# A transformer block on one core: three-tile units from the start, and the weight scaling moved to GpSimd

## The chip, the core and the metric

The kernel runs on one core of one Trainium2 chip. The metric is the time of one execution on the device, in microseconds (us). The engines are named as in the profile: PE (TensorE), DVE (VectorE), ACT (ScalarE), POOL (GpSimd) and SP (SyncE).

## What is computed

Four batches of 768 rows, 8 heads of 64. Attention is local: rows come in chunks of 32, and a chunk sees 8 memory keys, its own chunk, 16 rows to the left and 8 to the right. Behind it stands a feed-forward block with a layer norm and a residual.

```python
# attention, per chunk c of 32 rows (batch 4, heads 8, seq 768, dim 64, n_mem 8)
k_full = concat([mem_k, k[c*32-16 : c*32+32+8]])
a = softmax(q_c @ k_full.T / 8);  out_c = a @ v_full
# feed-forward on x = attention output, [4, 768, 512]
xn = (x - mean(x)) / sqrt(var(x) + 1e-6) * g_ln
out = x + max(xn @ w_ch1, 0) @ w_ch2          # 512 -> 2048 -> 512
```

## The kernel before

**Tiles and units.** A tile is 128 rows, so a batch has 6 tiles and the whole has 24. Feed-forward work goes by units of up to three tiles. A unit `u` has 16 *ups* (`up`, L308: four matmuls of 128 x (128 n) for n tiles, then a relu to `rT` on DVE, L316, for even chunks and on ACT, L314, for odd ones) and then, for each tile, four *down* groups (`down`, L325: four matmuls 128x512 each); behind the last group DVE scales by `rstd` and adds the residual (L332, `osb`), and SP writes the tile out. Step by step this makes 16 + 4n steps.

**Attention of a tile.** `scores` (8 matmuls, then two exp on ACT, L236), `values` (16 matmuls, then on DVE a reciprocal, a multiply to `xs`, bn_stats, bn_aggr, and the centred `xn` on DVE or POOL), `turn_x` (four transposes on PE and a copy to `xT`, L296) and `root` (two POOL operations that make `rstd`). It runs one unit ahead: `attend` puts these calls at steps of unit `u` for the tiles of unit `u + 1`. Keys and queries come in as rows and are transposed on PE by `kq_block(b, j, ...)`, four blocks a batch: a *turn* of 32 transposes (L181), key copies to `KT` on DVE (L196), query copies to `QZ` on ACT (L206). `scores` needs all four blocks.

**What sets the order.** The schedule is written by hand: the code order is each engine's order, and the `at(step, ...)` table interleaves attention, turns and loads with a unit's steps. PSUM has two `att` buffers (scores, values, turns of x, most key/query turns) and four `mm` buffers (ups, downs), taken in rotation. Loads with a cast go through POOL's queue (`load_kq`, `load_v_group`, `load_w1`, `load_w2`); in this queue each DMA waits for the eighth one before it to land.

**The start.** Batch 0 is loaded in two parts (rows up to 64 of each 96-row group, then the rest). The units are

```python
    units = [[0, 1, 2], [3], [4], [5]] + [[t, t + 1, t + 2] for t in range(6, 6 * B, 3)]
```

so the rest of batch 0 goes in three units of one tile. The layer norm's `g_ln` is multiplied into `w1` by `scale_w1(c, q)`, four operations of 128x512 for each quarter: quarter (0,0) on ACT ahead of unit 0, the others on DVE at steps 1, 5 and 9 of unit 0. Chunks 4 to 7 of the ups read quarter (0,1), 8 to 11 (1,0), 12 to 15 (1,1). `clear_v(1)` and `clear_kq(1)`, memsets of the second buffers, stand at steps 11 and 13 of unit 0. The second half of batch 0's turns stands at steps 18 to 21 of unit 0, whose down groups go part by part over the tiles. Batch 1 is loaded from step 24 of unit 0 on, batch 2's keys and queries at the end of unit 3.

Of the kernel before, what the change touches and what calls it, by code (L numbers as in the profile page):

```python
# [10 lines left out]
ACTF = mybir.ActivationFunctionType  # L11
ALU = mybir.AluOpType
# [3 lines left out]
def kernel(  # L16
# [12 lines left out]
    nc = tc.nc  # L29

    B, H, S, D = 4, 8, 768, 64
    FF = 2048
    NG = 12
# [104 lines left out]
    def load_w2(c):  # L138

        nc.gpsimd.dma_start(  # L140
            out=w2c[c], in_=dram(moe_w_ch2, c * 512 * 512, [[2048, 128], [1, 2048]])
        )

    def scale_w1(c, q, on_act=False):

        for dt in range(4):
            w = w1c[c][:, dt, 512 * q : 512 * q + 512]
            if on_act:
                nc.scalar.activation(out=w, in_=w, func=ACTF.Copy, scale=g_col[:, dt : dt + 1])  # L149
            else:  # L150
                nc.vector.tensor_scalar(
                    out=w, in0=w, scalar1=g_col[:, dt : dt + 1], scalar2=None, op0=ALU.mult
                )


# [46 lines left out]
    def keep_q(copy, pv, b, j, par, n, g0, g1):  # L202


        rows = slice(64 * par, 64 * par + 64)
        copy(  # L206
            out=free(QZ[b % 2][rows, j, g0, par, :], 0, [[128, g1 - g0], [8, 8], [1, 8]]),
            in_=free(pv[rows, :], 8 * g0, [[8, g1 - g0], [1, 8], [n, 8]]),
        )
# [13 lines left out]
    def scores(b, t):  # L223
        p = slot("att")
        a = AT[t % 3]
        for gg in range(2):
            g = 2 * t + gg
            for j in range(4):
                nc.tensor.matmul(  # L229
                    out=p[:, gg, 128 * j : 128 * j + 128],  # L230
                    lhsT=KT[b % 2][:, j, KR * g : KR * g + 128],
                    rhs=QZ[b % 2][:, j, g, :, :],
                    start=True, stop=True,
                )
        for c in range(2):
            nc.scalar.activation(  # L236
                out=free(a, 32 * c, [[512, 2], [64, 8], [1, 32]], KR),
                in_=free(p, 32 * c, [[512, 2], [64, 8], [1, 32]], KR),
                func=ACTF.Exp, bias=band[0:KR, c : c + 1], scale=0.125,
            )  # L240
# [97 lines left out]
    def clear_kq(i):  # L338
        nc.vector.memset(KT[i][:, :, 8:24], 0.0)
        nc.vector.memset(KT[i][:, :, NG * KR - 8 : KC], 0.0)  # L340
        nc.vector.memset(QZ[i][0:64, :, :, 1, :], 0.0)
        nc.vector.memset(QZ[i][64:128, :, :, 0, :], 0.0)
# [33 lines left out]
    nc.scalar.copy(out=memk16, in_=memk32)  # L376
    clear_v(0)
    clear_kq(0)
    v_mem(0)
    for g in range(4):  # L380
        load_v_group(0, g)
# [16 lines left out]
    for g in range(6, 8):  # L398
        load_v_group(0, g)
    load_w2(2)  # L400
    load_w2(3)
    for g in range(8, NG):
        load_v_group(0, g)

    first_k = [as16(slot("mm")[:, :]) for j in range(4)]
# [20 lines left out]
    turn_x(0, 0, 0, nc.scalar.copy)  # L426
    values(0, 2, 2, False)
    turn_x(0, 1, 1, nc.scalar.copy)
    scale_w1(0, 0, True)
    turn_x(0, 2, 2, nc.scalar.copy)  # L430
    for t in range(3):
        root(t, t)


    units = [[0, 1, 2], [3], [4], [5]] + [[t, t + 1, t + 2] for t in range(6, 6 * B, 3)]
    for u, tiles in enumerate(units):
        n = len(tiles)
# [6 lines left out]
        def attend(*steps, on_pool=True):  # L444

            for i, (s0, s1, s2) in enumerate(steps):
                t = following[i]
                at(s0, scores, t // 6, t % 6)
                at(s1, values, t // 6, t % 6, t % 9, on_pool)
                at(s2, turn_x, u + 1, i, t % 6)  # L450
                if not on_pool:
                    at(s2, root, t % 6, t % 9)

        if u == 0:
            for c in range(1, 4):
                at(4 * c - 3, scale_w1, c // 2, c % 2)
            at(11, clear_v, 1)
            at(13, clear_kq, 1)
            for j in range(4):
                at(18 + j, kq_block, 0, j, 6, NG, "att")  # L460
            attend((21, 21, 24), on_pool=False)
            for which in range(2):
                at(24, load_kq, 1, which)
            for g in range(2):
                at(25, load_v_group, 1, g)
        elif u == 1:
            at(0, mem_cols, 1)
            at(0, v_mem, 1)
            attend((1, 16, 19), on_pool=False)
            for g in range(2, 6):  # L470
                at(19, load_v_group, 1, g)
        elif u == 2:
            attend((1, 6, 15), on_pool=False)
            for j in range(4):
                at(16 + j, kq_block, 1, j, 0, NG, "att")
            for g in range(6, NG):
                at(18, load_v_group, 1, g)
        elif u == 3:
            attend((1, 12, 16), (6, 16, 18), (14, 17, 19), on_pool=False)
            for which in range(2):  # L480
                at(19, load_kq, 2, which)
        elif following:
            steps = [(1 + 7 * i, 5 + 7 * i, 11 + 7 * i) for i in range(3)]
            attend(*steps)
            if u in (4, 6):
                b = u // 2
# [7 lines left out]
            if u == 5:  # L494
# [42 lines left out]
```

## Time and profile before

| | |
|---|---|
| Time of three runs | 265.8, 267.0, 269.39 us; median 267.0 |
| Profiled execution | 265.7 us, of which the trace spans 263.8 |
| Busy time of PE, DVE, ACT, POOL | 225.6, 144.3, 92.6, 77.1 us |
| Mean granted clock of PE | 0.974 |
| Moved by DMA | 22.04 MB |

Rows of the profile name line, engine, operation and `out<-in`; `xN` is a count. In a row of the timeline the first two numbers are the start and the duration, and brackets give the engine's idle time just before and what ended it. In a row of waits stand the total, the count and the longest.

### The profile page before, as it was taken

Reading aid. Unit: us, or ns where it says so; the run is one execution under the profiler, and the core shown is the slowest. Engines: PE = TensorE matmul, PEld = TensorE weight load, DVE = VectorE, ACT = ScalarE, POOL = GpSimd, SP = SyncE. Lnnn points to the kernel's source line nnn. Section 1 sums busy time; section 2 is a strip of 40 time slices with the busy share of each in tenths; the row PEclk is TensorE's granted clock in tenths of the full one; section 3 lists DMA queues with packets and bytes.
Section 4 is the critical chain, followed back from the end, with each engine's and each line's share of the span. In section 5 each row is a group of like instructions: output and inputs, shape, how many; then the busy total and the mean of one; then the engine's idle time right before and its main releaser. Section 6 shows DMA issues by size and latency. Waiting matters only on the chain.

```text
span 263.8 us, 5638 instructions
## 1 busy us (share of the span) xinstructions
PE 225.6 (86%) x2340; PEld 142.6 (54%) x2340; DVE 144.3 (55%) x323; ACT 92.6 (35%) x174; POOL 77.1 (29%) x149
## 2 busy tenths in 40 slices
PE   0555796959987778796999999999999999999993
PEld 0443363534755475474557745765576466546641
DVE  4729376324567728666566643677655446454321
ACT  2065331340422772252544511535455025302300
POOL 7750251006067002647130324274012202220000
PEclk9999999777999979999999999999999999999999
DMA  6999999005999900499989116079310120021012
GB/s 73 161 152 213 209 184 94 2 0 73 219 183 70 91 2 0 73 176 112 92 114 233 24 41 101 12 47 101 82 42 1 42 80 0 2 80 42 0 40 80
DMA packets 44104, 22.04 MB, mean 84 GB/s; under 512 B 32896, under 2 KB 39424, under 8 KB 44032
## 3 DMA queue, kind: packets, MB, share of 16 engines
q0 software_dynamic: 39312, 14.39, 66.4%
q1 hardware_dynamic: 4768, 7.31, 9.6%
q8 instruction: 18, 0.29, 0.5%
q14 instruction: 6, 0.05, 0.1%
HBM read 28.84 MB, written 6.29 MB: 133 GB/s over the span
## 4 chain that ended last, share of the span: by engine, by line
PE 66%; DVE 13%; DMA 8%; ACT 7%; issue 3%; POOL 1%; ACTq 0%; DVEq 0%; POOLq 0%
PE mm L325 29%; PE mm L308 26%; DMA q<-in_q_dram 8%; PE att L229 3%; PE att L181 3%; ACT QZ L206 3%; PE att L248 3%; ACT AT L236 2%; DVE KT L196 2%; DVE xs L256 2%; DVE bst L263 2%; PE att L291 1%; ACT w1c L149 1%; DVE xn L275 1%; DVE rT L316 1%
## 5 line engine op out<-in xcount | busy, mean ns | idle before, releaser
L308 PE MATMUL mm<-xT,w1c 128*128 128x384 f16 (+1 forms) x640 | 94.5, 302 | 5.3 <-DVE xT L296 1.9
L325 PE MATMUL mm<-w2c,rT 128*128 128x512 f16 x384 | 93.0, 390 | 2.1 <-DVE rT L316 2.1
L308 PEld LDWEIGHTS <-w1c 128*128 128x128 f16 x640 | 62.5, 116 | 28.2 <-issue 8.2
L314 ACT ACTIVATE rT<-mm 128x384 f16<-128x384 f32 (+1 forms) x80 | 33.4, 425 | 101.1 <-PE mm L308 66.7
L325 PEld LDWEIGHTS <-rT 128*128 128x128 f16 x384 | 36.0, 100 | 41.5 <-issue 5.7
L316 DVE TENSOR_SCALAR rT<-mm 128x384 f16<-128x384 f32 (+1 forms) x80 | 37.4, 474 | 36.0 <-PE mm L308 34.6
L206 ACT COPY QZ<-att 64x768 f16<-64x768 f16 (+1 forms) x33 | 21.9, 667 | 41.2 <-DVE KT L196 24.8
L236 ACT ACTIVATE AT<-att,band 96x512 f16<-96x512 f32 x48 | 30.1, 678 | 7.5 <-PE att L229 7.3
L332 DVE SCALAR_TENSOR_TENSOR osb<-mm,rstd,xs 128x512 f32<-128x512 f32 x24 | 18.0, 750 | 23.6 <-PE mm L325 18.8
L266 POOL TENSOR_SCALAR nmean<-mv 128x1 f32<-128x1 f32 x15 | 2.9, 191 | 83.9 <-DVE mv L264 76.1
L229 PE MATMUL att<-QZ,KT 128*128 128x128 f16 x192 | 16.7, 233 | 6.7 <-ACT QZ L206 4.7
L296 DVE COPY xT<-att 128x512 f16<-128x512 f16 x21 | 8.9, 423 | 24.5 <-PE att L291 24.5
L196 DVE COPY KT<-att 128x80 f16<-128x80 f16 (+3 forms) x38 | 16.2, 479 | 10.3 <-PE att L181 8.1
L281 POOL TENSOR_SCALAR veps<-mv 128x1 f32<-128x1 f32 x24 | 6.5, 270 | 51.0 <-DVE mv L264 49.6
L108 POOL DMA_DIRECT2D V<-in_v_dram x24 | 18.5, 778 | 6.9 <-DMA w2c<-in_moe_w_ch_dram 4.1
L229 PEld LDWEIGHTS <-KT 128*128 128x128 f16 x192 | 14.0, 105 | 9.1 <-issue 6.6
L263 DVE BATCH_NORM_STATS2 bst<-xs 128x6 f32<-128x512 f32 x24 | 16.7, 694 | 0.8
L256 DVE TENSOR_TENSOR xs<-att,rec 128x512 f32<-128x512 f32 x24 | 16.6, 691 | 0.8
L181 PEld LDWEIGHTS <-k 96*64 96x64 f16 (+1 forms) x320 | 8.5, 121 | 13.6 <-DMA k<-in_k_dram 8.5
L291 PE MATMUL att<-identity,xn 128*128 128x128 f16 x96 | 10.1, 233 | 5.0 <-DVE xn L275 4.3
L248 PEld LDWEIGHTS <-AT 96*64 96x64 f16 x384 | 8.9, 118 | 9.6 <-issue 4.4
L285 POOL TENSOR_TENSOR rstd<-veps,mhalf 128x1 f32<-128x1 f32 x24 | 13.4, 556 | 2.0
(52 smaller groups left out, 130.9 us busy)
## 6 DMA issues: line engine op xcount, KB each, us to landing
out_dram<-osb SPq DMA_DIRECT2D x24, 256.0 KB, 2.5
V<-in_v_dram POOLq DMA_DIRECT2D x36, 96.0 KB, 6.2
k<-in_k_dram POOLq DMA_DIRECT2D x3, 768.0 KB, 9.4
q<-in_q_dram POOLq DMA_DIRECT2D x3, 768.0 KB, 14.6
w1c<-in_moe_w_ch_dram POOLq DMA_DIRECT2D x2, 1024.0 KB, 14.0
w2c<-in_moe_w_ch_dram POOLq DMA_DIRECT2D x4, 512.0 KB, 16.5
k<-in_k_dram POOLq DMA_DIRECT2D x1, 512.0 KB, 6.2
q<-in_q_dram POOLq DMA_DIRECT2D x1, 512.0 KB, 8.9
```

The source lines that it names most:

```text
L108: nc.gpsimd.dma_start(out=V[b % 2][r : r + hi - lo, g, :, 0:64], in_=dram(v, b * H * HS + lo * D, [[64, hi - lo], [HS, H], [1, 64]]),)
L196: nc.vector.tensor_copy(out=free(KT[b % 2], j * KC + 24 + 32 * ga + 8 * lo, [[KR, gb - ga], [8, m], [1, 8]]), in_=free(pv, lo, [[8, gb - g ...
L206: copy(out=free(QZ[b % 2][rows, j, g0, par, :], 0, [[128, g1 - g0], [8, 8], [1, 8]]), in_=free(pv[rows, :], 8 * g0, [[8, g1 - g0], [1, 8], ...
L229: nc.tensor.matmul(out=p[:, gg, 128 * j : 128 * j + 128], lhsT=KT[b % 2][:, j, KR * g : KR * g + 128], rhs=QZ[b % 2][:, j, g, :, :], start ...
L236: nc.scalar.activation(out=free(a, 32 * c, [[512, 2], [64, 8], [1, 32]], KR), in_=free(p, 32 * c, [[512, 2], [64, 8], [1, 32]], KR), func= ...
L256: nc.vector.tensor_tensor(out=x.rearrange("p (a h d) -> p a h d", a=2, h=4), in0=free(p, 0, [[512, 2], [HD, 4], [1, 64]]), in1=free(r, 0, ...
L263: nc.vector.bn_stats(out=bst[i], in_=x)
L308: nc.tensor.matmul(out=p, lhsT=free(w, i, [[4, 128]]), rhs=xT[u % 2][:, dt, 0 : 128 * n], start=(dt == 0), stop=(dt == 3),)
L314: nc.scalar.activation(out=o, in_=p, func=ACTF.Relu)
L316: nc.vector.tensor_scalar(out=o, in0=p, scalar1=0.0, scalar2=None, op0=ALU.max)
L325: nc.tensor.matmul(out=p, lhsT=rT[hc][:, 128 * i : 128 * i + 128], rhs=w2c[hc // 4][:, hc % 4, :], start=(hc == 0), stop=(hc == 15),)
L332: nc.vector.scalar_tensor_tensor(out=o, in0=p, scalar=rstd[t % 9], in1=xs[t % 9], op0=ALU.mult, op1=ALU.add,)
```

## The change

Units are three tiles from the first to the last, so there are eight instead of ten. In unit 0 the second half of batch 0's turns comes at steps 14 to 17, the attention of tiles 3, 4 and 5 at steps 18 to 27, and the down groups go tile by tile. In unit 1 batch 1's turns stand at steps 2, 5, 8 and 11, and the attention of tiles 6, 7 and 8 at steps 13 to 26. Three quarters of `w1` are scaled on POOL, between the loads of its queue. `clear_kq(1)` and `clear_v(1)` move ahead of unit 0. Batch 1's keys, queries and first six V groups are issued behind the roots of tiles 0 to 2; its other V groups and batch 2's keys and queries at steps 0 and 1 of unit 1.

```diff
-    def scale_w1(c, q, on_act=False):
+    def scale_w1(engine, c, q):
         for dt in range(4):
             w = w1c[c][:, dt, 512 * q : 512 * q + 512]
-            if on_act:
-                nc.scalar.activation(out=w, in_=w, func=ACTF.Copy, scale=g_col[:, dt : dt + 1])
+            g = g_col[:, dt : dt + 1]
+            if engine is nc.scalar:
+                nc.scalar.activation(out=w, in_=w, func=ACTF.Copy, scale=g)
             else:
-                nc.vector.tensor_scalar(
-                    out=w, in0=w, scalar1=g_col[:, dt : dt + 1], scalar2=None, op0=ALU.mult
+                engine.tensor_scalar(
+                    out=w, in0=w, scalar1=g, scalar2=1.0, op0=ALU.mult, op1=ALU.mult
                 )
...
     clear_kq(0)
+    clear_kq(1)
...
     load_w2(2)
+    scale_w1(nc.gpsimd, 0, 1)
     load_w2(3)
-    for g in range(8, NG):
+    scale_w1(nc.gpsimd, 1, 0)
+    load_v_group(0, 8)
+    scale_w1(nc.gpsimd, 1, 1)
+    for g in range(9, NG):
         load_v_group(0, g)
...
+    clear_v(1)
     scores(0, 0)
...
-    scale_w1(0, 0, True)
+    scale_w1(nc.scalar, 0, 0)
...
+    for which in range(2):
+        load_kq(1, which)
+    for g in range(6):
+        load_v_group(1, g)
...
-    units = [[0, 1, 2], [3], [4], [5]] + [[t, t + 1, t + 2] for t in range(6, 6 * B, 3)]
+    units = [[t, t + 1, t + 2] for t in range(0, 6 * B, 3)]
...
         if u == 0:
-            for c in range(1, 4):
-                at(4 * c - 3, scale_w1, c // 2, c % 2)
-            at(11, clear_v, 1)
-            at(13, clear_kq, 1)
             for j in range(4):
-                at(18 + j, kq_block, 0, j, 6, NG, "att")
-            attend((21, 21, 24), on_pool=False)
-            for which in range(2):
-                at(24, load_kq, 1, which)
-            for g in range(2):
-                at(25, load_v_group, 1, g)
-        elif u == 1:
-            at(0, mem_cols, 1)
-            at(0, v_mem, 1)
-            attend((1, 16, 19), on_pool=False)
-            ...
-        elif u == 2:
-            attend((1, 6, 15), on_pool=False)
-            for j in range(4):
-                at(16 + j, kq_block, 1, j, 0, NG, "att")
-            ...
-        elif u == 3:
-            attend((1, 12, 16), (6, 16, 18), (14, 17, 19), on_pool=False)
-            for which in range(2):
-                at(19, load_kq, 2, which)
+                at(14 + j, kq_block, 0, j, 6, NG, "att")
+            attend(((18, 20, 23), (20, 22, 25), (22, 24, 27)), on_pool=False)
+            at(26, mem_cols, 1)
+            at(26, v_mem, 1)
+        elif u == 1:
+            for j in range(4):
+                at(2 + 3 * j, kq_block, 1, j, 0, NG, "att")
+            for g in range(6, NG):
+                at(0, load_v_group, 1, g)
+            for which in range(2):
+                at(1, load_kq, 2, which)
+            attend(((13, 16, 20), (16, 18, 23), (20, 22, 26)))
...
                 i, part = divmod(step - 16, 4)
-                if u == 0:
-                    part, i = divmod(step - 16, n)
                 down(tiles[i], i, part)
```

On POOL, in the prologue, the queue of loads stood so before (`w2c_77` and `w2c_78` are the third and fourth part of `w2`, `V_83` is the V buffer of batch 0, `veps` and `rstd` belong to the roots):

```order
L140 DMA w2c_77<-in_moe_w_ch_dram 128x2048
L140 DMA w2c_78<-in_moe_w_ch_dram 128x2048
L108 DMA V_83<-in_v_dram 96x8x64 x3
L108 DMA V_83<-in_v_dram 80x8x64
L281 TENSOR_SCALAR veps_137<-mv_128 128x1
```

and with the change:

```order
L140 DMA w2c_77<-in_moe_w_ch_dram 128x2048
L152 TENSOR_SCALAR w1c_73<-w1c_73,g_col 128x512 x4
L140 DMA w2c_78<-in_moe_w_ch_dram 128x2048
L152 TENSOR_SCALAR w1c_74<-w1c_74,g_col 128x512 x4
L108 DMA V_83<-in_v_dram 96x8x64
L152 TENSOR_SCALAR w1c_74<-w1c_74,g_col 128x512 x4
L108 DMA V_83<-in_v_dram 96x8x64 x2
L108 DMA V_83<-in_v_dram 80x8x64
L282 TENSOR_SCALAR veps_137<-mv_128 128x1
```

Twelve operations have come in, between loads that stay in their order.

On DVE, in the prologue, the memsets of the first key and query buffers (`KT_85`, `QZ_87`) stood directly ahead of the first key copies:

```order
L339 MEMSET KT_85 128x4x8
L340 MEMSET KT_85 128x4x20
L341 MEMSET QZ_87 64x48x32
L342 MEMSET QZ_87 64x48x32
L196 COPY KT_85<-mm_154 128x72
```

and with the change those of the second buffers (`KT_86`, `QZ_88`) stand between:

```order
L340 MEMSET KT_85 128x4x8
L341 MEMSET KT_85 128x4x20
L342 MEMSET QZ_87 64x48x32
L343 MEMSET QZ_87 64x48x32
L340 MEMSET KT_86 128x4x8
L341 MEMSET KT_86 128x4x20
L342 MEMSET QZ_88 64x48x32
L343 MEMSET QZ_88 64x48x32
L197 COPY KT_85<-mm_154 128x72
```

They came from step 13 of unit 0.

On DVE, at the end of unit 0, the attention of tile 3 (its `xn_101`), the turned x, and the three outputs stood ahead of the first relu of the next unit (`rT_106`, one tile wide):

```order
L275 TENSOR_SCALAR xn_101<-xs_95,mv_131 128x512
L296 COPY xT_105<-att_151 128x4x128
L332 SCALAR_TENSOR_TENSOR osb_122<-mm_155,rstd_140,xs_92 128x512
L332 SCALAR_TENSOR_TENSOR osb_123<-mm_156,rstd_141,xs_93 128x512
L332 SCALAR_TENSOR_TENSOR osb_124<-mm_153,rstd_142,xs_94 128x512
L316 TENSOR_SCALAR rT_106<-mm_154 128x128
```

and with the change, from the end of tile 4's attention (`xn_102`) on:

```order
L276 TENSOR_SCALAR xn_102<-xs_96,mv_132 128x512
L333 SCALAR_TENSOR_TENSOR osb_123<-mm_156,rstd_141,xs_93 128x512
L297 COPY xT_105<-att_152 128x4x128
L256 RECIPROCAL rec_150<-att_151 128x8
L257 TENSOR_TENSOR xs_97<-att_151,rec_150 128x512
L264 BN_STATS bst_127<-xs_97 128x6
L265 BN_AGGR mv_133<-bst_127 128x2
L276 TENSOR_SCALAR xn_103<-xs_97,mv_133 128x512
L297 COPY xT_105<-att_152 128x4x128
L172 COPY KT_86<-memKT 128x4x12x8
L333 SCALAR_TENSOR_TENSOR osb_124<-mm_153,rstd_142,xs_94 128x512
L297 COPY xT_105<-att_151 128x4x128
```

The last turned x, which the next unit's first up needs, now stands behind the attention of two more tiles and behind the third output.

More of the change, by code (lines that the diff above doesn't have):

```diff
@@ L442, in at, with attend @@
             plan.setdefault(step, []).append((fn, args))
-        def attend(*steps, on_pool=True):
+        def attend(steps, on_pool=True):
             for i, (s0, s1, s2) in enumerate(steps):
@@ L454 @@
         if u == 0:
[L455 to L458 removed]
             for j in range(4):
[L460 to L481 removed]
+                at(14 + j, kq_block, 0, j, 6, NG, "att")
[7 more added lines that the diff above has]
+                at(0, load_v_group, 1, g)
+            for which in range(2):
+                at(1, load_kq, 2, which)
+            attend(((13, 16, 20), (16, 18, 23), (20, 22, 26)))
         elif following:
             steps = [(1 + 7 * i, 5 + 7 * i, 11 + 7 * i) for i in range(3)]
[L484 to L486 removed]
+            attend(steps)
+            if u in (2, 4):
+                b = u // 2 + 1
                 for j, step in enumerate((steps[1][1], steps[2][1], steps[2][1], 23)):
@@ L493 @@
                 at(22, v_around, b)
-            if u == 5:
+            if u == 3:
                 for which in range(2):
```

## The prediction

> **What bounds the kernel now.** I read the page's head first, then a table of stages, then the waits inside the worst stages.
>
> ```profile
> span 263.8 us, 5638 instructions
> PE 225.6 (86%) x2340; PEld 142.6 (54%) x2340; DVE 144.3 (55%) x323; ACT 92.6 (35%) x174; POOL 77.1 (29%) x149
> GB/s 73 161 152 213 209 184 94 2 0 73 219 183 70 91 2 0 73 176 112 92 114 233 24 41 101 12 47 101 82 42 1 42 80 0 2 80 42 0 40 80
> ```
>
> TensorE (PE) is busy for 86% of the span, so the question is where the other 14% lies, and whether the busy time is at full speed. The table has one stretch for each unit (its length, then the busy time of PE, weight loads, DVE, ACT and POOL with their instructions, then the granted clock, the DMA share and GB/s):
>
> ```profile
> 28.48:65.90 37.42, 32.35 (x268) 17.86 (x268) 18.66 (x45) 8.97 (x18) 9.60 (x16) 0.86 0.81 87
> 65.90:75.80 9.90, 8.53 (x109) 6.12 (x108) 6.61 (x18) 3.15 (x10) 1.57 (x3) 1.00 1.40 217
> 75.80:90.00 14.20, 12.08 (x236) 8.94 (x235) 9.11 (x24) 6.53 (x15) 8.18 (x12) 1.00 1.49 92
> 90.00:108.75 18.75, 13.38 (x171) 9.73 (x166) 12.31 (x31) 8.61 (x18) 3.80 (x7) 0.91 0.05 16
> 108.75:138.19 29.44, 27.41 (x325) 17.43 (x325) 17.65 (x38) 13.67 (x22) 13.33 (x24) 1.00 1.74 125
> 138.19:162.62 24.43, 24.43 (x198) 14.84 (x197) 12.71 (x26) 7.49 (x14) 6.40 (x14) 1.00 0.51 98
> 162.62:190.06 27.44, 27.30 (x327) 17.37 (x325) 18.00 (x39) 13.67 (x22) 9.41 (x18) 1.00 0.65 69
> ```
>
> The prologue ends at 28.48. The rows are unit 0, the three one-tile units, then three-tile units, in which PE is idle for almost nothing. So the kernel is PE-bound from 108.75 on and chain-bound before. Tiles 0 to 5 take 37.42 + 9.90 + 14.20 + 18.75 = 80.27 us.
>
> What six tiles cost when PE is full follows from the last unit, which has no attention beside it:
>
> ```profile
> 238.62:249.01 10.39, 10.39 (x65) 7.26 (x64) 5.11 (x9) 3.44 (x7) 0.00 (x0) 1.00 0.07 27
> 249.01:259.40 10.39, 10.37 (x49) 4.51 (x46) 1.50 (x2) 0.49 (x1) 0.00 (x0) 1.00 0.14 50
> ```
>
> Ups and downs of three tiles are 20.8 us (0.162 us and 0.216 us per matmul). The unit at 138.19 adds the attention of three tiles: 24.43 - 20.8 = 3.65. The unit at 162.62 adds four key/query turns: 27.44 - 24.43 = 3.0. So a unit with three tiles, three attentions and four turns is **27.4 us**; two of them are 54.9, against 80.27. The gap of 25 us is what the change can reach for. It consists of waits such as these two of the end of unit 0, and of half clock:
>
> ```profile
> PE mm L325 <- DVE rT L316: 2.1, 1, 2.1
> PE att L229 <- ACT QZ L206: 1.4, 1, 1.4
> ```
>
> ```profile
> 42.54:45.95 3.41, 1.31 (x11) 0.43 (x11) 1.90 (x2) 0.00 (x0) 0.00 (x0) 1.00 1.75 36
> 45.95:49.36 3.41, 3.41 (x52) 1.91 (x51) 0.67 (x2) 0.95 (x2) 0.00 (x0) 0.54 0.00 0
> 79.90:83.30 3.40, 1.95 (x25) 1.41 (x23) 2.57 (x8) 0.83 (x3) 2.51 (x4) 1.00 0.90 32
> ```
>
> A stretch of 3.41 us with 1.31 us of PE work is followed by one at clock 0.54; the one with 1.95 us of work held 1.00 (the columns are those of the stages).
>
> **The prologue.** `clear_kq(1)` and `clear_v(1)` come into it, on VectorE (DVE).
>
> ```profile
> 4.28 0.09 DVE L339 MEMSET KT<- 128x32 uint32 x1
> 6.42 1.34 DVE L342 MEMSET QZ<- 64x1536 uint32 x1 [0.36 <-issue]
> 9.22 3.11 DVE L196 COPY KT<-mm 128x72 f16<-128x72 f16 x8 [1.47 <-PE mm L181]
> 13.58 0.56 DVE L206 COPY QZ<-att 64x384 f16<-64x384 f16 x1 [0.55 <-ACT QZ L206]
> 19.52 0.21 DVE L255 RECIPROCAL rec<-att 128x8 f32<-128x8 f32 x1 [3.43 <-PE att L248]
> 38.79 0.48 DVE L346 MEMSET V<- 32x512 f16 x1
> ```
>
> `clear_kq(0)` lasted from 4.28 to 7.76, 3.48 us; the second one is queued right behind it, ahead of the KT copies. DVE had 1.47 us free there and 0.55 us before its first QZ copy; the rest, 3.48 - 1.47 - 0.55 = **1.45 us**, moves everything up to the first up. Bounds: 0 (the gaps swallow it) and 3.48. `clear_v(1)`, two memsets of 0.48 us and three shorter operations, stands where DVE idled 3.43 us, now 2.0 of them left; I charge nothing, and at most 0.5. Unit 0 then starts at 28.48 + 1.45 = 29.93.
>
> **Weight scaling.** Twelve DVE operations leave unit 0's up part and become twelve on GpSimd (POOL). The trace has none of that kind there; the nearest row is xn, of the same 128x512 size with f32 input. The other bound is the DVE price.
>
> ```profile
> L270 POOL TENSOR_SCALAR xn<-xs,nmean x15: 694/695/695, 115.9 to 234.0; 128x512 f16<-128x512 f32 x15
> L151 DVE TENSOR_SCALAR w1c<-w1c,g_col x12: 333/345/569, 30.4 to 37.9; 128x512 f16<-128x512 f16 x12
> 22.94 0.56 POOL L140 DMA_DIRECT2D w2c<-in_moe_w_ch_dram  x1 [3.74 <-DMA w1c<-in_moe_w_ch_dram]
> 27.84 0.55 POOL L140 DMA_DIRECT2D w2c<-in_moe_w_ch_dram  x1 [4.34 <-DMA w1c<-in_moe_w_ch_dram]
> 37.16 0.76 POOL L108 DMA_DIRECT2D V<-in_v_dram  x1 [1.77 <-DMA q<-in_q_dram]
> 28.48 12.55 PE L308 MATMUL mm<-xT,w1c 128*128 128x384 f16 x64 [1.29 <-ACT xT L296]
> ```
>
> I take 0.695. Weights land at 22.94 and 27.84. Group (0,1) is ready at 22.94 + 0.56 + 2.8 = 26.3; (1,0) at 27.84 + 0.55 + 2.8 = 31.2; (1,1), behind one V issue of 0.8, at 34.8. The up part took 12.55 us here against 10.39 in the last unit: its first dozen matmuls ran at half speed (the row gives +2.1, which stays). PE wants (0,1) four ups in, at 34.6, (1,0) at 37.2, (1,1) at 39.8. All are 5 us early, so this costs nothing; queued behind are three V issues and three roots, and the last V issue waited for q's landing until 37.16 anyway. From 1.24 us per operation the last group is late (24.9 + 12 x 1.24 = 39.8), and each further us costs 12.
>
> **Unit 0** (its start is 0). Work: 27.4 + 2.1 = 29.5. Two waits remain.
>
> ```profile
> 53.66 0.67 DVE L196 COPY KT<-att 128x352 f16<-128x352 f16 x2 [1.10 <-ACT QZ L206]
> 54.42 0.96 ACT L206 COPY QZ<-att 64x384 f16<-64x384 f16 x2 [0.81 <-DVE KT L196]
> 58.04 0.21 DVE L255 RECIPROCAL rec<-att 128x8 f32<-128x8 f32 x1 [3.71 <-PE att L248]
> 59.95 0.48 DVE L275 TENSOR_SCALAR xn<-xs,mv 128x512 f16<-128x512 f32 x1
> L236 ACT ACTIVATE AT<-att,band 96x512 f16<-96x512 f32 x48 | 30.1, 678 | 7.5 <-PE att L229 7.3
> L332 DVE SCALAR_TENSOR_TENSOR osb<-mm,rstd,xs 128x512 f32<-128x512 f32 x24 | 18.0, 750 | 23.6 <-PE mm L325 18.8
> L296 DVE COPY xT<-att 128x512 f16<-128x512 f16 x21 | 8.9, 423 | 24.5 <-PE att L291 24.5
> ```
>
> The last turn ends on PE near 17.5 (12.5 of ups, four turns of 0.75, two groups of four down matmuls of 0.86). KT and QZ copies of 0.67 and 0.96 follow one another, to 19.4, and the scores of tile 3 need them; PE has one down group and three score matmuls meanwhile and waits **0.9** (1.4 before). Then attention runs beside the downs, two down groups (1.7 us) to a step of it: exp of tile 3 (two of 0.68) to 21.2, its values at 21.8 behind two groups, the scores of tile 4 behind them, exp to 23.9, the values of tile 4 to 24.7. A tile costs DVE 2.4 us from reciprocal to xn (58.04 to 60.43), so that tile 3 is done by then. From 24.8 DVE's row holds, in the order shown with the change: 2.4, osb 0.75, xT 0.42, 2.4, xT 0.42, mem_cols about 0.35, osb 0.7, xT 0.42 = 7.9, to 32.7. PE's last down ends at 30.4, so it idles about **1.9** beside the last turn. Unit 0 lasts 32.7 us.
>
> **Unit 1** holds the same work, 27.3. Its turns lie in the up part, on full-size copies:
>
> ```profile
> L196 DVE COPY KT<-att 128x880 f16<-128x880 f16 x10 | 10.6, 1063 | 0.0
> L206 ACT COPY QZ<-att 64x768 f16<-64x768 f16 x20 | 15.9, 793 | 20.0 <-DVE KT L196 14.8 <-PE mm L308 5.1
> q<-in_q_dram POOLq DMA_DIRECT2D x1, 768.0 KB, 14.6
> 121.73 0.53 PE L181 MATMUL att<-identity,q 96*64 96x96 f16 x16 [2.03 <-DMA q<-in_q_dram]
> ```
>
> The fourth turn ends near 11.3 (twelve ups of 0.65, four turns, and 0.4 for ups behind a late rT); KT copies (1.06 and two short ones, some 1.4) and two QZ copies (1.6) lead to 14.4, while PE has two ups and three score matmuls, to 12.9: the scores of tile 6 wait 1.5. 27.3 + 1.5 + 0.4 = 29.2 us. Data: k and q of batch 1 are now issued near 41.6 us behind the roots, instead of at 61.9; 14.6 us to landing, and up to 5 us of older transfers ahead (the seventh slice of the GB/s row, to 46 us, is the last with traffic), give 56 to 61, and the first turn is due at 62.6 + 2 = 64.6. If that cover is gone, each us late is a us lost. Loads for batch 2 move from unit 3's end into unit 1's start, in front of POOL work that is due 15 us later, so the 2.03 us wait for q at 121.73 goes, and the unit behind it takes 27.4 like its sister at 162.62. SP only gets `v_mem(1)` earlier.
>
> **The sum.** 29.93 + 32.7 + 29.2 + 27.4 + (263.8 - 138.19 = 125.6) = 244.8. Clock: the 3.41 us ahead of unit 1 hold 1.1 + 0.25 = 1.35 us of PE work, like the 1.31 that was followed by clock 0.54. I charge one such stretch, 3.41/2 = 1.7: span 246.5. The profiled execution took 265.7, 1.9 over its span: 248.4. The median of the runs, 267.0, lies 1.3 above that execution; I add half: **249**.
>
> The Trainium skill, "TensorE: Matmul & The Clock Gate", Part 1, says that the clock is halved after an idle window of about 3.4 us, and advises only against gaps longer than that. The trace disagrees on the gap: the longest wait in the stretch before clock 0.54 was 2.1 us. By the page nothing is charged, and the sum is 247.3, which lies inside the forecast's own range.
>
> **Rivals.**
> - No cold stretch, and the prologue's gaps swallow the clear: 249 - 1.7 - 1.45 = 246, and 244 if half of the 4.3 us of waits goes. For it: the stretch with 1.95 us of work stayed warm, and where a stretch begins is chance. 20% for under 246.
> - The chains do not overlap: the three attentions of unit 0 run one behind another, since only two att buffers serve scores, values and turns. Before, tile 3 took from the last QZ copy (55.38) to its xn (60.43) 5.05 us, with the xT copy 5.5. Three of them from 19.4 end at 35.9 instead of 32.7: +3.2, and with a second cold stretch 254. For it: DVE already sets the end in my count; against: the unit at 162.62 hides the same work. 15%, from 252 to 256.
> - GpSimd's scaling is slow. It breaks even at (39.8 + 18 - 24.9)/12 = 2.7 us per operation, and is over 2% **slower** than 267 from 3.2 us: 273. Against: fifteen xn operations lie within 1 ns of 695 while DVE works. 4%; in between (1.5 to 2.4 us, 252 to 263) 3%. The Trainium skill, "GPSIMD Engine Reference", Key points, speaks for it: both engines share SBUF interfaces, and they contend when DVE runs in a two-port mode. The xn row shows no sign of it; no run here shows this operation.
> - The change doesn't fill PE: the matmuls go, the waits stay. PE was busy 32.35 + 8.53 + 12.08 + 13.38 = 66.3 of the 80.27 us, so 13.9 us of idle time would stand beside 54.9 + 2.1 of work: 70.9, 9.4 less than before; with the prologue's 1.45 that is 267 - 9.4 + 1.45 = 259. For it: those waits are chains of other engines, which the change moves but does not shorten. Against: counted one by one, 5 us of them are left. 6%.
>
> My forecast, 246 to 252, has 52%. The range 244 to 256 takes in half of the first rival's best cases and the second whole; it leaves out some 3% below and 13% above. A change of 2%, 5.3 us, is about what a measurement of this kernel can tell: faster 0.91, same 0.05, slower 0.04.
>
> **What would show it.** In the new trace: first up near 29.9; POOL's scaling at 0.7 us each, done by 35; PE's next unit near 62.6, with a wait on DVE xT ahead; its scores waiting on ACT QZ for 1.5; no wait for q; units of 24.3 to 27.4 after that. A first up part with waits on POOL, or a wait on k or q in unit 1, would make it wrong.

## The result, and the profile after

The changed kernel takes **247.81 us** (median of four executions, 247.22 to 248.02), against 266.44 for the kernel before beside it: ratio 0.928, 95% interval 0.922 to 0.935. The prediction was 249.0, with 244 to 256. One thing is needed to read the times and intervals below: of 25 executions of the kernel before that ran beside the experiments, five took 260.8 to 261.6 us with a mean granted clock of 1.00 and nearly all others 264 to 267 us with 0.97 to 0.99, so a ratio to it is uncertain by about 1%, and two profiled executions of variants in which PE was slow from end to end (782 and 388 us) are left out of the times. Differences between the variants are read from stages of their traces.

The head of the page of the changed kernel (the profiled execution took 248.02 us, 1.7 over its span):

```profile
span 246.3 us, 5335 instructions
PE 218.5 (89%) x2212; PEld 135.4 (55%) x2212; DVE 137.6 (56%) x292; ACT 90.6 (37%) x158; POOL 87.1 (35%) x167
```

PE is busy for 7.1 us less, with 128 matmuls fewer, and idle for 10.4 us less. The table of stages (prologue, unit 0, unit 1, unit 2, the rest; columns as in the prediction):

```profile
0.00:30.68 30.68, 10.82 (x216) 9.20 (x217) 21.31 (x49) 11.61 (x20) 20.20 (x41) 1.00 1.61 159
30.68:63.40 32.72, 30.88 (x324) 17.98 (x324) 17.10 (x38) 11.49 (x22) 18.68 (x31) 1.00 1.78 155
63.40:93.28 29.88, 28.41 (x324) 17.39 (x324) 17.48 (x37) 13.81 (x22) 10.92 (x21) 1.00 0.87 100
93.28:120.72 27.44, 27.30 (x325) 17.40 (x324) 18.19 (x39) 13.62 (x22) 11.72 (x21) 1.00 0.87 74
120.72:246.30 125.58, 121.06 (x1025) 73.47 (x1023) 63.51 (x129) 40.07 (x72) 25.58 (x56) 0.99 0.31 56
```

Tiles 0 to 5 take 32.72 + 29.88 = 62.60 us, against 80.27 before, a gain of 17.7. Unit 2 takes 27.44, against 29.44 before, a gain of 2.0. The prologue costs 2.2 more, and the rest is the same 125.6. That sums to 17.5, the difference of the spans. From the wait that ends at the first up to the end of unit 1, PE waits for only three things (line and releaser; total, count, longest; the one on ACT's xT is the wait ahead of the first up):

```profile
PE att L230 <- ACT QZ L207: 2.1, 2, 1.4
PE mm L309 <- ACT xT L297: 1.2, 1, 1.2
PE mm L309 <- DVE xT L297: 1.1, 1, 1.1
```

The waits on rT and q that the prediction shows of before are gone, the one on q with unit 2, in which PE idles for 0.14 us. Rows of DVE and POOL in the prologue, and behind them the two groups as a whole (count: shortest, median and longest in ns):

```profile
9.94 1.34 DVE L343 MEMSET QZ<- 64x1536 uint32 x1 [0.36 <-issue]
23.43 2.70 POOL L152 TENSOR_SCALAR w1c<-w1c,g_col 128x512 f16<-128x512 f16 x4
25.10 1.32 DVE L276 TENSOR_SCALAR xn<-xs,mv 128x512 f16<-128x512 f32 x1
28.24 0.57 DVE L276 TENSOR_SCALAR xn<-xs,mv 128x512 f16<-128x512 f32 x1
28.34 2.96 POOL L152 TENSOR_SCALAR w1c<-w1c,g_col 128x512 f16<-128x512 f16 x4
L152 POOL TENSOR_SCALAR w1c<-w1c,g_col x12: 682/684/947, 23.4 to 34.1; 128x512 f16<-128x512 f16 x12
L276 DVE TENSOR_SCALAR xn<-xs,mv x6: 486/488/1321, 22.8 to 61.4; 128x512 f16<-128x512 f32 x6
```

The second pair of clears ends at 11.28, as the prediction's 7.76 + 3.48 has it. POOL's scaling takes 0.684 each. But the xn of tile 1, which lasts 0.49 us elsewhere, lasted 1.32 while POOL scaled. A delay of that kind is not idle time of DVE: it stands in the duration of the operation itself, and only the spread between the median and the longest of a group shows it. The first up came at 30.68, not 29.93.

### The profile page after: what moved, and what is told of

It is laid out like the page before. It is cut to its first block, busy times and chain, and to the rows that moved or that the text cites. A ratio compares the mean times of both kernels' runs of the same rounds, so it can differ in the third digit from the quotient of the medians.

```text
span 246.3 us, 5335 instructions
## 1 busy us (share of the span) xinstructions
PE 218.5 (89%) x2212; PEld 135.4 (55%) x2212; DVE 137.6 (56%) x292; ACT 90.6 (37%) x158; POOL 87.1 (35%) x167
## 4 chain that ended last, share of the span: by engine, by line
PE 74%; DVE 14%; ACT 6%; issue 3%; POOL 1%; ACTq 0%; DVEq 0%; POOLq 0%
PE mm L309 34%; PE mm L326 28%; DVE KT L197 4%; PE att L230 4%; PE att L182 3%; PE att L249 3%; ACT QZ L207 3%; DVE xs L257 2%; DVE bst L264 2%; PE att L292 1%; ACT AT L237 1%; DVE QZ L343 1%; DVE QZ L342 1%; ACT w1c L150 1%; DVE xn L276 1%
## 5 line engine op out<-in xcount | busy, mean ns | idle before, releaser
L309 PE MATMUL mm<-xT,w1c 128*128 128x384 f16 x512 | 92.8, 333 | 2.4 <-ACT xT L297 1.2
L326 PE MATMUL mm<-w2c,rT 128*128 128x512 f16 x384 | 89.4, 379 | 0.0
L309 PEld LDWEIGHTS <-w1c 128*128 128x128 f16 x512 | 56.9, 116 | 28.1 <-issue 5.8
L315 ACT ACTIVATE rT<-mm 128x384 f16<-128x384 f32 x64 | 30.9, 490 | 86.3 <-PE mm L309 36.9
L326 PEld LDWEIGHTS <-rT 128*128 128x128 f16 x384 | 35.5, 98 | 37.0
L317 DVE TENSOR_SCALAR rT<-mm 128x384 f16<-128x384 f32 x64 | 34.9, 551 | 35.3 <-PE mm L309 35.3
L267 POOL TENSOR_SCALAR nmean<-mv 128x1 f32<-128x1 f32 x18 | 3.4, 191 | 101.7 <-DVE mv L265 90.0
L237 ACT ACTIVATE AT<-att,band 96x512 f16<-96x512 f32 x48 | 30.1, 678 | 13.2 <-PE att L230 13.1
L230 PE MATMUL att<-QZ,KT 128*128 128x128 f16 x192 | 16.2, 230 | 5.8 <-ACT QZ L207 2.9
L230 PEld LDWEIGHTS <-KT 128*128 128x128 f16 x192 | 13.5, 103 | 8.5 <-issue 5.4
L286 POOL TENSOR_TENSOR rstd<-veps,mhalf 128x1 f32<-128x1 f32 x24 | 13.3, 556 | 2.0
L271 POOL TENSOR_SCALAR xn<-xs,nmean 128x512 f16<-128x512 f32 x18 | 12.5, 694 | 1.8
## 6 DMA issues: line engine op xcount, KB each, us to landing
k<-in_k_dram POOLq DMA_DIRECT2D x3, 768.0 KB, 10.4
q<-in_q_dram POOLq DMA_DIRECT2D x3, 768.0 KB, 13.3
w1c<-in_moe_w_ch_dram POOLq DMA_DIRECT2D x2, 1024.0 KB, 13.6
```

The costliest lines, as they stand in the source:

```text
L230: nc.tensor.matmul(out=p[:, gg, 128 * j : 128 * j + 128], lhsT=KT[b % 2][:, j, KR * g : KR * g + 128], rhs=QZ[b % 2][:, j, g, :, :], start ...
L237: nc.scalar.activation(out=free(a, 32 * c, [[512, 2], [64, 8], [1, 32]], KR), in_=free(p, 32 * c, [[512, 2], [64, 8], [1, 32]], KR), func= ...
L309: nc.tensor.matmul(out=p, lhsT=free(w, i, [[4, 128]]), rhs=xT[u % 2][:, dt, 0 : 128 * n], start=(dt == 0), stop=(dt == 3),)
L315: nc.scalar.activation(out=o, in_=p, func=ACTF.Relu)
L317: nc.vector.tensor_scalar(out=o, in0=p, scalar1=0.0, scalar2=None, op0=ALU.max)
L326: nc.tensor.matmul(out=p, lhsT=rT[hc][:, 128 * i : 128 * i + 128], rhs=w2c[hc // 4][:, hc % 4, :], start=(hc == 0), stop=(hc == 15),)
```

## The experiments

**1. What lengthens xn?** The scaling back on VectorE, at steps 1, 5 and 9 of unit 0, with all else as changed:

```diff
-    scale_w1(nc.gpsimd, 0, 1)
...
-    scale_w1(nc.gpsimd, 1, 0)
-    load_v_group(0, 8)
-    scale_w1(nc.gpsimd, 1, 1)
...
+            for c in range(1, 4):
+                at(4 * c - 3, scale_w1, nc.vector, c // 2, c % 2)
```

> The changed kernel, with the three quarters scaled on DVE again, at steps 1, 5 and 9 of unit 0 as before. Theory A (moving the scaling to POOL freed nothing that PE waited for, and cost 0.8 us by the long xn): the first up starts near 29.9, the ups of unit 0 keep their pace, since each group of four takes DVE 1.3 us where it idles 0.7 to 2.0 between relus and four mm buffers cover the rest; span some 0.8 below the changed kernel. Rival B (the move relieved DVE on the path): PE waits for relus in unit 0's ups by up to 2 us, span 1 to 2 us above the changed kernel.

Measured: 247.13 us (246.61 to 247.47). Its group of xn and its stages up to unit 1:

```profile
L276 DVE TENSOR_SCALAR xn<-xs,mv x6: 485/486/488, 22.8 to 59.8; 128x512 f16<-128x512 f32 x6
0.00:29.84 29.84, 10.82 (x216) 9.20 (x217) 20.39 (x49) 11.60 (x20) 15.10 (x33) 1.00 1.62 157
29.84:61.80 31.96, 30.12 (x325) 17.75 (x325) 20.04 (x50) 11.47 (x22) 15.57 (x26) 1.00 1.79 165
```

No xn is longer than 0.488 us, and the first up is at 29.84. So 0.84 us of the prologue belonged to POOL's scaling, and the scaling on DVE costs unit 0 nothing either: PE did not wait for rT. (Unit 0 is 0.76 shorter than in the changed kernel, but its first 60 matmuls alone took 11.65 us against 12.42.) Moving the scaling to POOL therefore gained nothing here.

The next kernel keeps the scaling on POOL but begins it behind the last load of w2, so that tile 1's xn has no company. It ran twice:

```diff
-    scale_w1(nc.gpsimd, 0, 1)
     load_w2(3)
+    scale_w1(nc.gpsimd, 0, 1)
     scale_w1(nc.gpsimd, 1, 0)
```

> The changed kernel, with POOL's first four scaling operations put behind the load of the last part of w2 instead of ahead of it, so that POOL is idle from 23.4 to 28.3 us, while DVE makes the xn of tiles 1 and 2. Theory A, that POOL's scaling holds up DVE's xn (1.32 us instead of 0.49): all xn of the prologue take 0.49, the first up starts near 29.9 instead of 30.68, the span falls by 0.8 to some 245.5. Rival B, that the long xn has another cause (the loads that land in the same microseconds, or ACT): xn stays at 1.3 and the first up at 30.7. In either case the weights come in time, (0,1) at 31.0, (1,0) at 33.7, (1,1) at 37.3, against the first up at 29.9 with chunks 4, 8 and 12 wanted at 35.2, 37.8 and 40.4.

> GpSimd's first scaling behind the load of w2 once more, for a profile at full clock. If the held-up xn is GpSimd's scaling beside it, every xn of unit 0 is at 0.49 us and the first up at 29.9. If the third xn runs into GpSimd's scaling row now, it takes longer than 1 us, and where it waits for the row's end up to 5 us, and the first up is at 30.7 or later.

Measured: 246.35 us in the first run (three executions, 246.29 to 247.28), but 251.92 in the profiled execution of the second. Its rows on DVE, POOL and PE:

```profile
27.41 6.51 DVE L276 TENSOR_SCALAR xn<-xs,mv 128x512 f16<-128x512 f32 x1
27.54 5.36 POOL L152 TENSOR_SCALAR w1c<-w1c,g_col 128x512 f16<-128x512 f16 x8
32.85 0.84 POOL L108 DMA_DIRECT2D V<-in_v_dram  x1
33.98 0.61 PE L292 MATMUL att<-identity,xn 128*128 128x128 f16 x4 [7.73 <-DVE xn L276]
```

The third xn began 0.13 us before a row of eight scalings, and ended 0.2 us after the V issue that follows them: 6.51 us for 0.49 us of work. The trace of the first run has the same picture on DVE and POOL (5.76 us). Of the two readings the second came true, and went beyond its 5 us. Since the timed executions of the first run lie 5.6 us lower, xn probably got through there; no trace shows that. This place is no safer than the changed kernel's: a longer row is a longer possible wait.

Last of this group, POOL's work made three times as long, by two multiplications by 1 ahead of each scaling:

```diff
+                for extra in range(2):
+                    engine.tensor_scalar(
+                        out=w, in0=w, scalar1=1.0, scalar2=1.0, op0=ALU.mult, op1=ALU.mult
+                    )
                 engine.tensor_scalar(
```

> The changed kernel, with two more POOL operations of the same size (times one) ahead of each scaling operation, so that a group of four takes 8.2 us instead of 2.7. Theory of the prediction (POOL only has to deliver in time): (0,1) is ready at 31.6, (1,0) at 40.4, (1,1) at 49.4, and chunks 8 and 12, wanted at 38.5 and 41.1, wait on POOL: about 8 us more, as waits of PE inside the ups, first up where it was. Theory A (a DVE operation from SBUF to SBUF that starts in a closed row of POOL operations waits for the row's end): xn of tile 1 or 2 ends with POOL's first row near 31.7 instead of 26.4, the next one with the second row near 40 or later; the first up starts at 41 to 42 instead of 30.7, and PE hardly waits inside the ups; 10 to 12 us more. bn_stats, reciprocal and the memsets keep their times.

Measured: 258.64 us (258.55 to 258.74). Waits of PE, and two rows of it:

```profile
PE mm L313 <- POOL w1c L156: 6.9, 5, 1.7
39.01 0.35 PE L313 MATMUL mm<-xT,w1c 128*128 128x384 f16 x1 [1.69 <-POOL w1c L156]
L280 DVE TENSOR_SCALAR xn<-xs,mv x6: 486/487/623, 22.8 to 71.9; 128x512 f16<-128x512 f32 x6
```

Some 10.8 us more than the changed kernel, where about 8 was expected: the prediction's rival of a slow GpSimd is a real mechanism. By its formula, with the last group ready at 50.2 instead of 39.8, it is 10.4. Of the 10.8, 6.9 are PE's waits; most of the rest is half clock, as PE was busy in unit 0 for 35.16 us at a mean clock of 0.84, against 30.88 at 1.00. And xn was hardly delayed (0.62 at most), though the row on POOL was longer than ever. So "xn waits for the end of the row" is refuted as a rule.

The traces show two outcomes. Either xn gets in between two of POOL's operations and takes 0.49 to 1.09 us, and POOL's row grows by 0.2 to 0.3 (2.96 us for the four from 28.34 above, against 2.70 for those from 23.43). Or POOL's row keeps its length, and xn ends only 0.2 to 0.3 us behind the row or the issue that follows it: so the 6.51 here, and so the 1.32 in the changed kernel, which ended at 26.42, behind a row that ended at 26.13. What decides between the two stays open.

**2. What do the clears cost?** `clear_kq(1)` split in two halves, at steps 1 and 3 of unit 0 (`clear_half` issues the same memsets, one of QZ in each half):

```diff
     clear_kq(0)
-    clear_kq(1)
...
+            at(1, clear_half, 1, 0)
+            at(3, clear_half, 1, 1)
```

> The changed kernel, with the memsets of the second key and query buffers taken out of the prologue and put at steps 1 and 3 of unit 0 on DVE, one QZ memset at each. If the 1.45 us that the prologue is charged for them is right, the first up starts 1.45 us earlier, near 29.2, minus what a changed overlap of xn and POOL's scaling does (0 to 0.8 either way), and the span falls to 244 to 245.5. Rival: DVE's gaps swallow the memsets anyway, or their place in unit 0 delays relus by as much: no change within 0.5 us.

Measured: 246.63 us (246.34 to 247.65); first up at 29.21, 1.47 earlier than in the changed kernel, and unit 0 is no longer for it:

```profile
29.21:62.06 32.85, 31.02 (x324) 17.91 (x324) 19.91 (x42) 11.48 (x22) 20.20 (x34) 1.00 1.73 167
12.51 1.92 PE L182 MATMUL att<-identity,q 64*64 64x64 f16 x64 [1.78 <-DMA q<-in_q_dram]
```

The 1.47 is not the clear alone: 0.64 of it is the second xn, which took 0.68 here and 1.32 there, so moving the clears gave 0.83. Without the clears, the landing of q sets the prologue again: PE's turn of q started at 12.51 here and at 11.97 in the kernel before, 0.54 later, and 28.48 + 0.54 + 0.19 (the rest of the xn delay) is the 29.21. So two limits stand close together: DVE's clears, and the landing of q, which came between 11.2 and 13.1 in these traces. The price of the clears is their distance. From the turn of q to the first xn it is 9.46 us where q sets the prologue (11.97 to 21.43 in the kernel before, 12.51 to 21.97 here), and with the clears in front that xn starts at 22.79; so, as an estimate from these rows, they cost 0.3 to 2.2 us by the landing of q.

**3. Units, or the small edits?** The kernel before, with its one-tile units, but with the scaling on POOL and the clears ahead:

```diff
     clear_kq(0)
+    clear_kq(1)
...
+    scale_w1(0, 1)
     load_w2(3)
-    for g in range(8, NG):
+    scale_w1(1, 0)
+    load_v_group(0, 8)
+    scale_w1(1, 1)
+    for g in range(9, NG):
...
+    clear_v(1)
     scores(0, 0)
```

> The kernel before, with its one-tile units and its load places, but with the other two parts of the change: three quarters of w1 scaled on POOL between the loads, and the memsets of the second buffers in the prologue. Theory A (the gain is the units'): the prologue costs 1.5 to 2.2 us, the 2.1 us wait for rT behind the memsets goes and with it at most the half-clock stretch behind it (1.7 us); the span stays within 3 us of 263.8, and the three one-tile units keep 9 to 10, 14 and 18 to 19 us. Rival B (DVE's scaling and memsets were what held unit 0 up, and its chain passed the delay on): unit 0 falls from 37.4 to 32 and the span by over 5 us.

Measured: 265.0 us (264.04 to 266.88), ratio 1.012 with 0.999 to 1.024. Its unit 0, its one-tile units, and the wait for q in the unit behind them:

```profile
30.68:63.92 33.24, 30.27 (x269) 16.74 (x268) 11.20 (x24) 8.96 (x18) 12.64 (x21) 0.95 0.80 78
63.92:73.83 9.91, 8.51 (x110) 6.12 (x109) 6.59 (x18) 3.14 (x10) 1.60 (x3) 1.00 1.20 227
73.83:88.04 14.21, 12.12 (x237) 8.94 (x236) 9.16 (x24) 6.57 (x15) 8.12 (x12) 1.00 1.82 98
88.04:106.89 18.85, 13.09 (x169) 9.47 (x166) 12.28 (x31) 8.55 (x18) 3.80 (x7) 0.91 0.04 16
120.21 0.53 PE L181 MATMUL att<-identity,q 96*64 96x96 f16 x16 [2.36 <-DMA q<-in_q_dram]
```

Unit 0 gains 4.2 us, since the wait for rT and part of the half clock go. The three one-tile units keep their times to 0.1 us (before: 9.90, 14.20, 18.75). All that the edits gained in the trace was given back: 2.2 us in the prologue, 0.6 in the first three-tile unit (a wait for q again) and 1.7 behind it, where the last unit had a mean clock of 0.95; why isn't known. Without the new units, and the loads and turns that were placed for them, the small edits show no gain.

**4. Did the earlier loads matter?** Batch 1's keys, queries and first V groups at steps 24 and 25 of unit 0, instead of behind the roots:

```diff
-    for which in range(2):
-        load_kq(1, which)
-    for g in range(6):
-        load_v_group(1, g)
...
+            for which in range(2):
+                at(24, load_kq, 1, which)
+            for g in range(6):
+                at(25, load_v_group, 1, g)
```

> The changed kernel, with batch 1's keys, queries and first six V groups issued at steps 24 and 25 of unit 0, as before, instead of behind the roots of tiles 0 to 2. Theory (the early issue is what makes room for the turns in unit 1): k is issued near 60 us, q lands 13 to 15 us after its issue, near 75, while the first turn is due at 65.4; PE waits 8 to 10 us, goes to half clock behind it (1.7 more), and the span is 8 to 12 us above the changed kernel. Rival (the turns are late on ACT and DVE anyway): under 4 us.

Measured: 254.66 us (254.27 to 255.06). The issues, and PE in unit 1:

```profile
55.69 0.82 POOL L99 DMA_DIRECT2D k<-in_k_dram  x1
56.51 0.77 POOL L99 DMA_DIRECT2D q<-in_q_dram  x1
69.58 0.85 PE L182 MATMUL att<-identity,q 96*64 96x96 f16 x16 [4.51 <-DMA q<-in_q_dram]
70.36 4.03 PE L309 MATMUL mm<-xT,w1c 128*128 128x384 f16 x12
62.50:99.52 37.02, 31.06 (x324) 18.44 (x324) 17.48 (x37) 13.92 (x22) 13.01 (x25) 0.91 1.82 127
```

That is 6.9 us more than the changed kernel, short of the expected 8 to 12, as the loads were issued some 4 us earlier than expected. Unit 1 takes 37.02 instead of 29.88: 4.5 us of waiting for q, 13 us after its issue, and some 2.6 more of busy time, as the wait was followed by matmuls at half speed (12 matmuls of ups in 4.03 us, against 2.14). So this wait cost half as much again as it shows.

Batch 2's keys and queries at step 27 of unit 1, instead of step 1. This kernel also ran twice:

```diff
-                at(1, load_kq, 2, which)
+                at(27, load_kq, 2, which)
```

> The changed kernel, with batch 2's keys and queries issued at step 27 of unit 1 instead of step 1. Theory: the wait for q before the first turn of unit 2 comes back with the 2.03 us that it had before, unit 2 takes 29.4 instead of 27.4, the span 2 us more. Rival: the queue is emptier now (six V groups have left it), q lands in time, and nothing changes.

> Batch 2's key and query loads at step 27 of unit 1 once more, for a profile at full clock. If a load issued that late doesn't land in time, PE waits for q at the turn of batch 2 by about 2 us and unit 2 is 29.4 or more. If it lands within 12 us of the issue, as batch 1's did, unit 2 is 27.4 and the span 246.

Measured: 247.60 us in the first run (three executions, 247.02 to 247.62), and 247.59 in the second; the time of the changed kernel. The issue, PE in unit 2, and, last, the same load in the kernel before, issued at 108.82 (size, and us from issue to landing):

```profile
92.61 0.77 POOL L99 DMA_DIRECT2D q<-in_q_dram  x1
103.85 0.53 PE L182 MATMUL att<-identity,q 96*64 96x96 f16 x16 [0.27 <-DMA q<-in_q_dram]
92.62:120.31 27.69, 27.42 (x326) 17.45 (x325) 18.12 (x39) 13.60 (x22) 13.20 (x23) 1.00 1.94 130
q<-in_q_dram POOLq DMA_DIRECT2D x1, 768.0 KB, 12.9
```

Here q is issued at the start of unit 2, as in the kernel before (92.61 and 92.62, against 108.82 and 108.75). It landed 11.2 us after its issue, and PE waited 0.27 us of the 2.03 that it did in the kernel before, where the landing took 12.9 (and 13.2 in the trace of experiment 3). So the reason that the prediction gave, an earlier issue, is worth 0.3 us of the 2.0 that unit 2 gained; the rest is that the transfer lands faster. Why it took longer before wasn't tried, and scatter isn't excluded.

**5. The two waits that are left.** Batch 1's turns two steps earlier in unit 1:

```diff
-                at(2 + 3 * j, kq_block, 1, j, 0, NG, "att")
+                at(3 * j, kq_block, 1, j, 0, NG, "att")
```

> The changed kernel, with batch 1's turns at steps 0, 3, 6 and 9 of unit 1 instead of 2, 5, 8 and 11. If the wait of 1.4 us of tile 6's scores is the latency of the fourth turn's KT and QZ copies, it goes to about 0.1, since two more ups (1.3 us) stand between; unit 1 falls from 29.9 to some 28.6 and the span by 1.3. Rival: ACT's queue is full with query copies and relus, and the wait only moves to ups that wait for relus: unit 1 stays at 29.5 to 29.9.

Measured: 246.09 us (246.01 to 247.26). The wait for QZ in unit 1 is gone (one of 0.7 is left, in unit 0), and the unit is 1.37 shorter:

```profile
PE att L230 <- ACT QZ L207: 0.7, 1, 0.7
62.79:91.30 28.51, 28.34 (x324) 17.41 (x324) 17.48 (x37) 13.48 (x22) 10.79 (x20) 1.00 0.94 105
```

The end of unit 0: the memory columns of unit 1 at step 19, and the outputs of tiles 1 and 2 on DVE behind the last xT copy.

```diff
-        if part == 3:
+        if part == 3 and t not in (1, 2):
...
-            at(26, mem_cols, 1)
+            at(19, mem_cols, 1)
...
+            if u == 0 and step == 27:
+                finish(1, down_slot[1])
+                finish(2, down_slot[2])
```

> Only the end of unit 0 is ordered otherwise: memory columns of unit 1 at step 19, and the outputs of tiles 1 and 2 on VectorE behind the last transposed copy. If VectorE's chain bounds the first up of unit 1, that chain is 1.6 us shorter, the last down matmul and its turn bound it then, and the unit ends 0.9 us sooner: unit 0 31.8, span 245.4. If TensorE bounds it, or unit 1 waits for the moved outputs instead, unit 0 and unit 1 together stay at 62.6 and the span at 246.3.

Measured: 246.71 us (246.24 to 247.07). PE's last rows of unit 0, and the first of unit 1:

```profile
59.25 1.89 PE L333 MATMUL mm<-w2c,rT 128*128 128x512 f16 x8
60.98 0.39 PE L292 MATMUL att<-identity,xn 128*128 128x128 f16 x4
61.88 2.11 PE L309 MATMUL mm<-xT,w1c 128*128 128x384 f16 x12 [0.52 <-DVE xT L297]
```

From the first turn on, unit 0 takes 61.88 - 42.25 = 19.63 us, against 63.40 - 43.03 = 20.37 in the changed kernel: 0.74 of the expected 0.9. What is left is PE's turn and DVE's copy behind the last down. Another 0.56 us of the unit is the cold start: its first 60 matmuls took 11.86 here and 12.42 there.

**6. All together.** The clears moved, the turns early, the end of unit 0 reordered, POOL's scaling behind the loads of w2, and, as the only new edit, ACT's scaling ahead of the copy of tile 1's xT:

```diff
+    scale_w1(nc.scalar, 0, 0)
     turn_x(0, 1, 1, nc.scalar.copy)
-    scale_w1(nc.scalar, 0, 0)
```

> The edits that single runs favour, put together: GpSimd's scaling behind the load of w2, the clears of batch 1's key and query buffers on VectorE at steps 1 and 3 of unit 0, batch 1's turns at steps 0, 3, 6 and 9 of unit 1, ScalarE's scaling of w1's first block ahead of a copy that waits, and at the end of unit 0 the memory columns at step 19 and the outputs of tiles 1 and 2 behind the last transposed copy. If the gains add: first up matmul near 28.4 (29.21 with the clears moved, 0.2 for the held-up xn, 0.6 for ScalarE's scaling in its idle time), unit 0 near 31.9, unit 1 28.5, unit 2 27.4, rest 125.6, so a span of 241.8 and a time of 243.6 us. If they don't, the third xn of the prologue falls beside GpSimd's scaling row again and waits for it up to 5 us, or TensorE's last down matmul ends the unit in place of VectorE: first up 30 or later, unit 0 at 32.7, and a span of 245 to 247.

Measured: **242.28 us** (six executions, 242.02 to 243.72), ratio to the kernel before 0.919, 0.912 to 0.926; 5.5 us below the median of the changed kernel, which was measured in another series. Its stages, and PE's turn of q:

```profile
0.00:27.10 27.10, 10.85 (x217) 9.11 (x218) 17.54 (x45) 11.60 (x20) 14.49 (x32) 1.00 1.64 154
27.10:58.75 31.65, 30.39 (x325) 17.90 (x324) 18.82 (x41) 11.48 (x22) 23.48 (x38) 1.00 1.74 174
58.75:87.33 28.58, 28.41 (x325) 17.41 (x324) 18.58 (x39) 13.48 (x22) 11.26 (x22) 1.00 0.80 114
87.33:114.76 27.43, 27.29 (x326) 17.39 (x324) 18.19 (x39) 13.60 (x22) 11.68 (x21) 1.00 0.80 72
11.17 1.91 PE L182 MATMUL att<-identity,q 64*64 64x64 f16 x64 [0.63 <-DMA q<-in_q_dram]
```

The gains add. The first up came 1.3 us before the expected 28.4; 0.8 of it is q, whose turn began 0.8 earlier than in the kernel before, by the landing's chance. The third xn ran from 25.24, ahead of POOL's row at 28.11, and so all six took 0.49.

## Why the prediction was right, and where its terms were off

- **Six tiles at 27.4 us a unit plus counted waits: right.** 32.7 and 29.2 were predicted, 32.72 and 29.88 measured, and 27.4 and 125.6 met. The rival in which the waits stay (259) fell, as did the one in which the chains of unit 0 don't overlap (254): PE waited only 1.8 us in unit 0 behind the first up. That the units, with the loads placed for them, carry the gain is shown by experiments 3 and 4.
- **Unit 0 came out by two errors that cancel.** PE's busy time was 30.88 us where 29.5 was charged. Of these 1.4, 0.6 are the cold start: the first 60 matmuls took 12.42 us, where 60 x 0.162 + 2.1 is 11.8. The other 0.8 lie in the part where turns and downs alternate, and weren't traced further. PE's waits were 0.74 and 1.09 where 0.9 and 1.9 were charged. DVE's chain did set the end, as the reordered end of experiment 5 shows, but PE's last down ended 1.5 us before it instead of 2.3. (By the prediction's own terms that down ends at 30.0, not 30.4, since the 29.5 hold the 0.4 of the last turn already; its end of the unit, from DVE's chain, doesn't depend on it.)
- **Unit 1 was 0.7 short.** The wait on QZ was 1.38 (1.5 predicted). The mis-sized term is "0.4 for ups behind a late rT": PE's busy time is 28.41, 1.1 over unit 2's 27.30, and it stays at 28.34 with the turns moved. So it goes with the ups among the turns, not with the wait: 12 matmuls of ups took 2.04 to 2.24 us there, from their start to the next row's, against 1.95 to 1.98 in unit 2. What lengthens them wasn't tried.
- **The clear: right.** 1.45 predicted; the changed kernel's prologue without POOL's scaling beside it begins unit 0 at 29.84, 1.36 later than before. That it came so close is in part luck: it holds for the landing of q at 11.97 in the trace of before, and by the estimate of experiment 2 another landing makes it anything from 0.3 to 2.2.
- **The scaling: its price was right, its side effect was missed.** 0.684 us each against 0.695, and ready 5 us ahead of PE. But the prediction looked for contention on the side of POOL, whose xn rows were even, and the one that paid was DVE: +0.75 us in the prologue. The Trainium skill, "SBUF — State Buffer", Who interferes with whom, says that a GpSimd operation and a vector `tensor_scalar` in a two-port mode exclude each other, that whoever issues first holds the ports for its whole instruction, and that the other fully blocks. The direction agrees with 1.32 us against 0.49; the size does not, as the 6.51 us in the second trace of the later scaling outlasted eight GpSimd instructions and one DMA issue. Nor does the order: by the profile that xn had begun 0.13 us ahead of the row. No row shows in which mode xn ran.
- **Loads: right in sum.** No wait for q or k in unit 1, and as experiment 4 shows, that is because they are issued by 42 us; at 56.5 the price is about 7 us. In the changed kernel q was issued at 41.15 and took 13.3 to land, so it was there by 54.5, ahead of the predicted 56 to 61.

**The cold stretch is the one term that wasn't there.** The prediction charges 1.7 us for a stretch ahead of unit 1 with 1.35 us of PE work. The stretches of 3.41 us on both sides of that boundary:

```profile
59.99:63.40 3.41, 2.32 (x16) 1.02 (x14) 3.25 (x8) 0.00 (x0) 1.89 (x4) 1.00 0.45 106
63.40:66.81 3.41, 3.41 (x48) 2.40 (x48) 1.57 (x4) 0.49 (x1) 3.41 (x5) 1.00 1.15 135
```

The first held 2.32 us of work, and the clock stayed at 1.00, in line with the 1.95 us that held it before. The failed step is the count of PE's work in it: 1.1 of downs and 0.25 of the turn, where 1.89 and 0.40 stood. The 1.7 were offset by 0.75 of contention in the prologue and 0.7 in unit 1, so that the spans agree (246.5 predicted, 246.3 measured) is luck: the errors cancel; the half of 1.3 us that was added for the median was not needed, as the median lies 0.2 below the profiled execution.

The clock is a part of the gain nevertheless. The kernel before had 0.86 in unit 0 and 0.91 in its last one-tile unit, the changed one 1.00 in units 0 to 2. At a mean clock of 1.00 the kernel before needed some 261.4 us. So, if those executions differ in nothing else, about 5 of the 18.6 us are half clock, and 13.6 the waits and the matmuls themselves; the prediction didn't split them.

## What to carry to other kernels

Price a restructured stage by the steady stage of the same trace that holds the same work, then add the waits one by one with their chains; here that gave five stages to within 0.8 us. When work moves to GpSimd, look at the durations of the vector engine's own operations beside it, not only at its idle time, and put a long row of such work where no vector operation of the critical chain falls. Before charging a cold clock, count PE's busy time in the stretch, and remember that a wait long enough to cool it costs more than its length (7.1 us for a wait of 4.5 here).

## What the runs showed of the hardware that was not expected

- A vector operation of 0.49 us (128x512, f32 to f16, both in SBUF) took 0.49 to 6.51 us beside GpSimd's scaling, while `bn_stats` (0.69), operations that read PSUM (0.69 and 0.56) and memsets (1.34) did not change. GpSimd's operation went from 0.684 to 0.97 at most where xn got in between.
- The first 60 matmuls of unit 0 took 11.65 to 12.56 us from trace to trace, whatever stood ahead of them, so up to 0.9 us of a comparison of two single traces is the cold start.
